# A planned attention, gated MLP and SoLU chain: slot 0 gated in one, one pair's exponentials set by set, ten weight blocks' low bits on ScalarE

## The chip, the cores and the metric

One NeuronCore of a Trainium2 chip runs the whole kernel. The metric is the device time of one execution in microseconds (us). Engines are TensorE (PE, with its weight loads as PEld), VectorE (DVE), ScalarE (ACT), GpSimd (POOL) and SyncE (SP), whose queue issues nearly all DMAs.

## The reference, cut to what matters

Three stages follow one another, for 2304 tokens of 512 features:

```python
attn = softmax(where(mask, q @ k.T / 8, -1e9)) @ v        # 4 x 8 heads, 576 positions, head size 64
x = attn as (2304, 512)                                   # plain heads: a window of 32; the others: every 4th of 128
xn = x / sqrt(mean(x * x) + 1e-6) * rms_g
g, val = xn @ w_gate, xn @ w_val                          # 512 x 1536 each
y = (silu(g) * val) @ w_out                               # 1536 x 512
h = y @ w_in                                              # 512 x 1024
solu = h * softmax(h); ln = layernorm(solu) * g_ln        # over 1024
out = ln @ w_out2                                         # 1024 x 512
```

The weights come as float64 and are turned into float32 on the chip.

## The kernel before, in words

**Tiling.** The tokens are cut into nine *pieces* of 256 (`PIECES`, L29). Pieces 0 and 1 are part 0 (512 tokens), piece 2 is part 1, and parts 2, 3 and 4 have two pieces each (`PARTS`, L34). The MLP has twelve *slots* of 128 hidden features (`f`, of `NF1`); a slot has three weight blocks of 128 x 512: gate (0), value (1), output (2). Every product is made of three float32r matmuls, high x high, high x low, low x high (`mm3`, L951), so each operand is split into a high part (a cast) and a low part (the difference).

**Who sets the order.** Nothing is ordered by hand, but for the last stages. Every step is entered with `plan.add(name, {engine: cost}, emit, needs, takes, uses, due)` (L201): engines that may run it with an estimated cost, the steps it needs, the buffers it takes, a due time. `Plan.order` (L210) plays this forward and picks, on the engine that is free first, the step with the smallest due time among those that can start within `SLACK` of the earliest. `NUDGE` (L110) shifts due times by name, `ENGINE` (L147) fixes an engine where several may serve. The instructions are then issued in that order (L1876), and on the chip each engine runs its own in order. Where the plan has TensorE idle before `FILL` = 75 us (L878), `fill` (L347) puts in matmuls on a constant tile that keep it busy and compute nothing.

**Weights.** `prepare` (L358) makes the steps of a slot: `fetch` (DMA of 512 KB per block), `shifted` (ScalarE, on the float64's high word, L386), `parts` (VectorE, the top three bits of the low word, L391), `joined` (VectorE, L395: both into one float32), `halves` (ScalarE, the cast), `lows` (VectorE or GpSimd, the difference). Slots below `SINGLE` = 7 do this block by block, the others all three blocks in one operation.

**Attention of the first two pieces.** `pair(t, m)` (L463), for t and m of 0 and 1, makes: `load_qk`, `load_v`, `scores` (32 matmuls and one that adds the mask, L493), `maximum`, `centred` (subtracts the maximum, on TensorE through an identity, L522, or on VectorE, L519), `exps` (one exponential over 128 x 512, L526), `sums` (L529), `norm`, `weights`, `transposes`, `turned0` and `turned1` (two copies out of PSUM, by `put`, L333 or L339), `values`. Then `rms(t)` (L767): `square`, `total` (matmuls with ones, L820), `eps`, `root` (GpSimd), `diag` (two operations, L858), `spread` (a matmul, L863), `keep` (piece 0), `scale`, `high` (L333 or L337) and `low` (L342). The other seven pieces go through `attention` (L599), later and beside the MLP; their `exps` is one exponential with an accumulated sum for each set of 64 keys (L660). Their `rms` adds the squares on GpSimd and then multiplies the sum by a matrix of ones (`mean`, L827, one float32 matmul of 256 columns in the code).

**The MLP.** `VIRTUAL` (L169) lists what `mlp` (L956) is called for: with `HALVES` = 1, slot 0 is done for piece 0 alone (v = 0), then for piece 1 alone (v = 1), each with gate and value products (`into`, L970), `tanh`, `silu`, `prod`, `uhigh`, `ulow` and output product (`outs`, L1012) over 256 tokens; slots 1 to 11 of part 0 are done over 512 tokens (v = 2); v = 3 and 4 are parts 1 and 2. The last two parts go together through Strassen-like products (`joint`, L1090), and the last stage works on pairs of 128-token rows (`second_stage`, L1708). `PACE` (L153) says after which gate product each later attention unit may start.

## Time and profile before

| | |
|---|---|
| runs of the kernel before | 711.76 us, median of 3 (711.76 to 712.01) |
| the profiled execution's own time | 712.27 us |
| its span in the trace | 710.2 us |
| TensorE, VectorE, ScalarE, GpSimd busy | 702.3, 509.4, 358.9, 135.5 us |

The span runs from the first to the last recorded instruction; the execution's own time has some 2 us more around it. A busy TensorE says that matmuls were under way, also those of `fill`. In the trace a matmul's record is longer than the distance to the next one's start, since matmuls overlap; that distance is what one costs in a dense run. Helpers issue instructions for many steps: L333, L337 and L339 are `put` (on ScalarE and VectorE), L342 is `less`.

### The profile page before, as it was taken

The numbers are of one execution on the slowest core, as the hardware profiler recorded it, in microseconds if no ns is written. First come the engines' busy times: TensorE is split into PE (matmuls) and PEld (weight loads), VectorE is DVE, ScalarE is ACT, GpSimd is POOL, SyncE is SP. The second block draws the span as 40 slices with busy tenths as digits, with TensorE's granted clock in tenths as the row PEclk, the third lists the DMA queues.
The fourth block names the chain that finished last, engine by engine and source line by source line (L and its number), as shares of the span: only waits on it lengthen the run. The fifth ranks groups of instructions, "written<-read, shape, count | busy, mean of one in ns | idle before, by whom it ended". The sixth has DMA issues, their size and how long they took to land.

```text
span 710.2 us, 11738 instructions
## 1 busy us (share of the span) xinstructions
PE 702.3 (99%) x4533; PEld 593.3 (84%) x4533; DVE 509.4 (72%) x932; ACT 358.9 (51%) x769; POOL 135.5 (19%) x166
## 2 busy tenths in 40 slices
PE   8999999999999999999999999999999999999998
PEld 6788888899998888888888888888888888888887
DVE  5899899679585986668966766689677677665552
ACT  2976854344535554516655554355375555543440
POOL 0322432250506121110000000014044311010110
PEclk9999999999999999999999999999999999999999
DMA  9999433154368764403321112947032111000001
GB/s 336 401 407 354 133 101 118 64 185 141 134 225 293 276 206 141 141 7 125 123 72 37 52 60 97 344 139 220 1 119 75 60 60 45 30 16 30 30 30 45
DMA packets 42424, 97.21 MB, mean 137 GB/s; under 512 B 3841, under 2 KB 14081, under 8 KB 42369
## 3 DMA queue, kind: packets, MB, share of 16 engines
q1 hardware_dynamic: 40640, 93.33, 37.9%
q10 hardware_dynamic: 1728, 3.15, 1.2%
q8 instruction: 35, 0.57, 0.3%
q14 instruction: 21, 0.16, 0.1%
HBM read 72.87 MB, written 23.59 MB: 136 GB/s over the span
## 4 chain that ended last, share of the span: by engine, by line
PE 93%; DMA 5%; ACT 1%; DVE 1%; SPq 0%; issue 0%; ACTq 0%
PE y L952 7%; PE ca L1292 7%; PE y L954 7%; PE y L953 7%; PE o L1689 5%; PE o L1688 5%; PE o L1687 5%; PE g L952 4%; PE vp L952 4%; PE g L953 4%; PE g L954 4%; PE vp L954 4%; PE vp L953 4%; DMA raw<-w 3%; PE cd L1292 2%; PE cb L1292 2%
## 5 line engine op out<-in xcount | busy, mean ns | idle before, releaser
L342 POOL TENSOR_TENSOR w<-wf,w 128x512 fp32r<-128x512 f32 (+1 forms) x15 | 25.1, 1673 | 203.9 <-ACT w L333 203.9
L1687 PE MATMUL o<-w,lt 128*128 128x512 f32 (+1 forms) x152 | 58.9, 388 | 0.0
L1689 PE MATMUL o<-w,lt 128*128 128x512 f32 (+1 forms) x152 | 57.6, 379 | 0.0
L1688 PE MATMUL o<-w,lt 128*128 128x512 f32 (+1 forms) x152 | 57.5, 379 | 0.0
L952 PE MATMUL y<-uh,w 128*128 128x512 f32 (+1 forms) x148 | 53.2, 359 | 0.0
L954 PE MATMUL y<-uh,w 128*128 128x512 f32 (+1 forms) x148 | 51.7, 349 | 0.0
L953 PE MATMUL y<-uh,w 128*128 128x512 f32 (+1 forms) x148 | 51.7, 349 | 0.0
L660 ACT ACTIVATE s<-s,nm 128x64 f32<-128x64 f32 x120 | 40.1, 337 | 18.6 <-DVE nm L655 18.6
L333 ACT CAST w<-wf 128x512 fp32r<-128x512 f32 (+1 forms) x40 | 28.3, 728 | 25.5 <-DVE wf L395 11.5
L952 PE MATMUL g<-xh,w 128*128 128x512 f32 (+1 forms) x104 | 40.4, 389 | 0.0
L333 ACT CAST uh<-u 128x512 fp32r<-128x512 f32 (+1 forms) x37 | 19.9, 537 | 38.3 <-DVE u L996 37.7
L953 PE MATMUL g<-xl,w 128*128 128x512 f32 (+1 forms) x104 | 39.0, 375 | 0.2 <-DVE xl L342 0.2
L952 PE MATMUL vp<-xh,w 128*128 128x512 f32 (+1 forms) x100 | 39.0, 390 | 0.0
L954 PE MATMUL g<-xh,w 128*128 128x512 f32 (+1 forms) x104 | 38.9, 374 | 0.0
L954 PE MATMUL vp<-xh,w 128*128 128x512 f32 (+1 forms) x100 | 38.2, 382 | 0.0
L953 PE MATMUL vp<-xl,w 128*128 128x512 f32 (+1 forms) x100 | 38.1, 381 | 0.0
L805 POOL TENSOR_TENSOR sq<-x 128x256 f32<-128x256 f32 x28 | 17.8, 647 | 105.7 <-DVE x L337 61.6
L1655 POOL TENSOR_SCALAR st<-st 128x1 f32<-128x1 f32 x18 | 8.7, 484 | 140.5 <-ACT sq L1646 140.3
L992 DVE SCALAR_TENSOR_TENSOR u<-u,g 128x512 f32<-128x512 f32 (+1 forms) x37 | 21.5, 582 | 18.3 <-ACT u L986 18.3
L986 ACT ACTIVATE u<-g 128x512 f32<-128x512 f32 (+1 forms) x37 | 19.0, 514 | 27.9 <-PE g L954 27.2
L1689 PEld LDWEIGHTS o<-w,lt 128*128 128x128 f32 x152 | 28.6, 188 | 5.3
L342 DVE TENSOR_TENSOR lt<-tp,lt 128x512 fp32r<-128x512 f32 x36 | 23.2, 684 | 13.6 <-ACT lt L333 13.6
(290 smaller groups left out, 2056.5 us busy)
## 6 DMA issues: line engine op xcount, KB each, us to landing
raw<-w SPq DMA_DIRECT2D x36, 512.0 KB, 9.1
es<-ec SPq DMA_DIRECT2D x12, 512.0 KB, 3.1
sc<-es SPq DMA_DIRECT2D x12, 512.0 KB, 3.4
qk<-qk SPq DMA_DIRECT2D x7, 800.0 KB, 5.5
vt<-v SPq DMA_DIRECT2D x10, 512.0 KB, 5.6
wo<-w SPq DMA_DIRECT2D x9, 512.0 KB, 7.6
wst<-wo SPq DMA_DIRECT2D x9, 512.0 KB, 3.7
yT<-yo SPq DMA_DIRECT2D x16, 256.0 KB, 3.1
```

The costliest lines, as they stand in the source:

```text
L333: nc.scalar.copy(dst, src) if scale is None else nc.scalar.mul(dst, src, scale)
L342: ENG[e].tensor_tensor(dst, a, b, ALU.subtract)
L660: nc.scalar.activation(T[s_][:, i], T[s_][:, i], AF.Exp, bias=st["nm"][:, i:i + 1], accum_out=sm[:, i:i + 1])
L952: nc.tensor.matmul(acc, wh, xh, start=first, stop=False)
L953: nc.tensor.matmul(acc, wh, xl, start=False, stop=False)
L954: nc.tensor.matmul(acc, wl, xh, start=False, stop=last)
L986: return lambda e: nc.scalar.activation(new(up, ("u", v, f), [P, 512])[:, 0:n], T["g", v, f], AF.Tanh, scale=0.5)
L992: return lambda e: nc.vector.scalar_tensor_tensor(out=u_of(f), in0=u_of(f), scalar=1.0, in1=T["g", v, f], op0=ALU.add, op1=ALU.mult)
L1292: nc.tensor.matmul(acc(x), w, y, start=not more and j == 0 and n == 0, stop=j == 1 and n == 2, skip_group_check=True)
L1687: nc.tensor.matmul(o, lt[:, 0, k], w[:, 0], start=(k == 0), stop=False)
L1688: nc.tensor.matmul(o, lt[:, 0, k], w[:, 1], start=False, stop=False)
L1689: nc.tensor.matmul(o, lt[:, 1, k], w[:, 0], start=False, stop=(k == NF2 - 1))
```

## The change

`HALVES` and the virtual tiles 0 and 1 are gone: slot 0 of part 0 belongs to v = 2. Its gate and value products run piece by piece (`by_piece`), the rest of the slot over 512 tokens. Pair (0, 0) scales its negated maximum by 1/8 on ScalarE and takes eight exponentials with accumulated sums; it has no `centred` and no `sums`. The mask's matmul is a step of its own (`masked`). `parts` may run on ScalarE, as one multiplication with a bias that rounds to the same three bits. Weights go block by block for slots 0 and 1, blocks 0 and 1 together for slots 2 to 6, all three from slot 7 on. `mean` of pieces 2 to 8 splits the sum of squares into high and low and uses two float32r matmuls. Estimated costs are changed in many places, the due times of a great many steps too (`NUDGE` grows from some 130 entries to some 270), `PACE` lets several attention units start earlier, and a few buffers of the last stages move (`units`, `H_AT`). Of `NUDGE` only the entries that the text speaks of stand here.

```diff
-HALVES = 1
+BY_SET = ((0, 0),)
...
-SINGLE = 7
+APART, WIDE = 2, 7
+
+
+def cuts(f):
+    return [(0,), (1,), (2,)] if f < APART else [(0, 1), (2,)] if f < WIDE else [(0, 1, 2)]
...
-         ('landed', 6): -22, ('load_qk', (1, 1)): -1.6, ('load_v', (0, 0)): 3.07, ('low', 0, 1): -43.6,
+         ('keep', 0): -197, ('landed', 6): -22, ('load_qk', (1, 1)): -1.6, ('load_v', (0, 0)): 1.8,
+         ('load_v', (0, 1)): 0.3, ('low', 0, 1): -43.6, ('low', 1, 0): -8, ('low', 1, 1): -32.8,
...
 ENGINE = {('copy', (3, 0)): 'd', ('copy', (5, 0)): 'd', ('copy', (7, 0)): 'd', ('copy', (7, 1)): 'd',
-          ('copy', (8, 1)): 'a', ('ecomb', 0): 'p', ('ecomb', 1): 'p', ('ecomb', 11): 'd', ('ecomb', 8): 'p',
-          ((1, 4), 'lows', 0): 'p', ((1, 6), 'lows', 1): 'p'}
+          ('copy', (8, 0)): 'a', ('copy', (8, 1)): 'a', ('diag', 0): 'a', ('ecomb', 0): 'p', ('ecomb', 1): 'p',
+          ('ecomb', 11): 'd', ('ecomb', 2): 'p', ('ecomb', 4): 'p', ('ecomb', 7): 'p', ('ecomb', 8): 'p',
+          ('high', 0, 0): 'a', ('high', 0, 1): 'a', ('keep', 0): 'a', ('low', 0, 0): 'p', ('low', 1, 0): 'd',
+          ('reload', 4): 'a', ('s5', 2): 'a', ('sumlow', 4): 'p', ('sums', 3): 'd', ('turned0', (1, 0)): 'a',
+          ('turned1', (1, 1)): 'a', ('u2', 2): 'a', (('in', 0), 't1'): 'p', (('in', 0), 't2'): 'd',
+          (('in', 0), 't4'): 'd', (('in', 1), 'lows', 't1'): 'p', (('in', 1), 'lows', 't3'): 'p',
+          (('in', 1), 't1'): 'd', (('in', 1), 't3'): 'p', ((1, 0), 'lows', 2): 'p', ((1, 0), 'parts', 0): 'a',
+          ((1, 0), 'parts', 1): 'a', ((1, 1), 'parts', 2): 'a', ((1, 2), 'parts', 0): 'd', ((1, 4), 'lows', 0): 'p',
+          ((1, 4), 'parts', 0): 'd', ((1, 7), 'lows', 0): 'p', ((1, 7), 'parts', 0): 'a', ((1, 8), 'parts', 0): 'a',
+          ((1, 9), 'lows', 0): 'p'}
...
-VIRTUAL = [(0, 0, 256, range(HALVES)), (0, 256, 256, range(HALVES)), (0, 0, 512, range(HALVES, NF1)),
-           (1, 0, 256, range(NF1)), (2, 0, 512, range(NF1))]
+VIRTUAL = {2: (0, 0, 512, range(NF1)), 3: (1, 0, 256, range(NF1)), 4: (2, 0, 512, range(NF1))}
...
         def parts(c):
-            return lambda e: nc.vector.tensor_scalar(word(c, 0).bitcast(U32), word(c, 0).bitcast(U32), 29, None,
-                                                     ALU.logical_shift_right)
+            def emit(e):
+                x = word(c, 0).bitcast(U32)
+                if e == "a":
+                    nc.scalar.activation(x, x, AF.Identity, scale=2.0 ** -29 * (1 - 2.0 ** -16), bias=down)
+                else:
+                    nc.vector.tensor_scalar(x, x, 29, None, ALU.logical_shift_right)
+            return emit
...
-            plan.add((key, "parts", n), {"d": one}, parts(c), [(key, "fetch", i) for i in c], due=due)
+            plan.add((key, "parts", n), {"d": one, "a": act}, parts(c), [(key, "fetch", i) for i in c], due=due)
...
         def exps(e):
-            nc.scalar.activation(T[s_], T[sp], AF.Exp, scale=0.125)
+            if K not in BY_SET:
+                nc.scalar.activation(T[s_], T[sp], AF.Exp, scale=0.125)
+                return
+            new(stg, s_, [P, 8, 64], name="s")
+            nc.scalar.mul(st["nm"], st["nm"], 0.125)
+            sm = small("sm")
+            for i in range(8):
+                nc.scalar.activation(T[s_][:, i], T[sp][:, i], AF.Exp, scale=0.125, bias=st["nm"][:, i:i + 1], accum_out=sm[:, i:i + 1])
...
         def mean(e):
             x = bank(a_mean, [P, TP], "ms")
-            nc.tensor.matmul(x, ones, T["sq", t, ks[0]], start=True, stop=True)
+            for h in range(2):
+                nc.tensor.matmul(x, ones_r, T["sqh" if h == 0 else "sql", t], start=h == 0, stop=h == 1)
+
+        def sum_high(e):
+            put(e, new(at, ("sqh", t), [P, TP], F32R, name="sqh"), T["sq", t, ks[0]])
+
+        def sum_low(e):
+            less(e, new(at, ("sql", t), [P, TP], F32R, name="sql"), T["sq", t, ks[0]], T["sqh", t])
...
-            plan.add(step("mean"), {"t": 0.45}, mean, [step("add", ks[-1]), ("ones",)], takes=[("a", a_mean)],
+            plan.add(step("sumhigh"), {"a": 0.42}, sum_high, [step("add", ks[-1])], takes=[("sq", ("sqh", t))],
                      uses=[("sq", t, ks[0])], due=due)
+            plan.add(step("sumlow"), {"p": 0.8, "d": 0.4}, sum_low, [step("sumhigh")], takes=[("rs", ("sql", t))],
+                     uses=[("sq", t, ks[0]), ("sqh", t)], due=due)
+            plan.add(step("mean"), {"t": 0.25}, mean, [step("sumlow"), ("onesr",)], takes=[("a", a_mean)],
+                     uses=[("sqh", t), ("sql", t)], due=due)
...
-                    alone = v == 4 and f == 0 and part == 0
-                    plan.add(name, {"t": cost}, by_piece(part, f, (key, v, f), i) if alone else into(part, f, (key, v, f), ks),
...
+                    alone = f == 0 and (v == 2 or v == 4 and part == 0)
+                    if alone and part == 1:
+                        before = [("g", v, f, i)] + ([(key, v, f, 0)] if i else [])
+                    plan.add(name, {"t": 1.44 if alone else cost}, by_piece(part, f, (key, v, f), i) if alone else into(part, f, (key, v, f), ks),
...
```

## Rows read from the trace of the kernel before

**Rows 1.** The page: busy time by engine; TensorE's granted clock in forty slices.

```profile
PE 702.3 (99%) x4533; PEld 593.3 (84%) x4533; DVE 509.4 (72%) x932; ACT 358.9 (51%) x769; POOL 135.5 (19%) x166
...
PEclk9999999999999999999999999999999999999999
```

**Rows 2.** Stretches: length, busy us (count) of PE, PEld, DVE, ACT, POOL; clock, DMA.

```profile
10.00:20.00 10.00, 8.59 (x144) 5.86 (x144) 8.91 (x19) 4.64 (x9) 0.00 (x0) 1.00 1.04 392
20.00:30.00 10.00, 9.22 (x127) 8.11 (x122) 8.31 (x21) 9.72 (x20) 2.31 (x2) 1.00 1.03 405
30.00:37.00 7.00, 6.35 (x50) 5.45 (x50) 5.85 (x12) 6.33 (x13) 3.33 (x3) 1.00 1.03 397
37.00:50.00 13.00, 13.00 (x81) 11.67 (x80) 12.60 (x21) 8.81 (x16) 3.98 (x3) 1.00 1.03 407
50.00:80.00 30.00, 30.00 (x216) 24.71 (x215) 28.34 (x44) 21.85 (x44) 8.35 (x6) 1.00 0.75 283
```

**Rows 3.** Groups by shape, TensorE to 75 us: the fills.

```profile
L351 PE MATMUL warm<-seed 128*128 128x256 bf16 x50 | 8.3, 323 | 0.9 <-POOL half L1870 0.9
...
L351 PE MATMUL rs<-seed 128*128 128x256 bf16 x19 | 2.5, 275 | 0.0
```

**Rows 4.** TensorE's waits from 36 us on: sum, times, longest.

```profile
PE tp L675 <- DVE s L668: 0.5, 1, 0.5
PE g L953 <- DVE xl L342: 0.2, 1, 0.2
```

**Rows 5.** Timeline of TensorE at piece 2's mean: start, length, what.

```profile
107.42 0.39 PE L954 MATMUL y<-uh,w 128*128 128x512 f32 x1
107.65 0.59 PE L827 MATMUL ms<-sq,ones 128*128 128x256 f32 x2
107.89 0.58 PE L952 MATMUL g<-xh,w 128*128 128x512 f32 x1
108.31 0.39 PE L953 MATMUL g<-xl,w 128*128 128x512 f32 x1
```

**Rows 6.** Timeline of TensorE in slot 0's first output product.

```profile
39.52 0.28 PE L952 MATMUL y<-uh,w 128*128 128x256 f32 x1
39.64 0.28 PE L953 MATMUL y<-uh,w 128*128 128x256 f32 x1
```

**Rows 7.** Timelines of the four engines in the ramp, by time.

```profile
10.27 0.67 DVE L529 TENSOR_REDUCE sm<-s 128x8 f32<-128x512 f32 x1
...
16.67 1.15 PE L566 MATMUL pv<-xp,qkv 128*64 128x64 f32 x32 [1.25 <-DMA qkv<-v]
...
17.85 0.69 ACT L386 ACTIVATE raw<-raw 128x512 f32<-128x512 f32 x1 [1.88 <-DMA raw<-w]
...
18.41 0.68 ACT L333 ACTIVATE xp<-tp,half 128x512 f32<-128x512 f32 x1
...
24.81 0.48 DVE L858 TENSOR_SCALAR rd<-ident,r 128x128 f32<-128x128 f32 x2 [0.60 <-POOL r L853]
...
30.85 1.57 DVE L858 TENSOR_SCALAR rd<-ident,r 128x128 f32<-128x128 f32 x2 [0.25 <-POOL r L853]
...
30.87 1.28 POOL L342 TENSOR_TENSOR xl<-xp,xh 128x512 fp32r<-128x512 f32 x1
...
34.69 0.68 ACT L386 ACTIVATE raw<-raw 128x512 f32<-128x512 f32 x1 [0.38 <-DMA raw<-w]
...
35.92 1.29 DVE L342 TENSOR_TENSOR xl<-x,xh 128x512 fp32r<-128x512 f32 x2 [0.71 <-ACT xh L333]
```

**Rows 8.** Groups by shape, 10 to 100 us: count, busy us, mean ns of one.

```profile
L386 ACT ACTIVATE raw<-raw 128x512 f32<-128x512 f32 x21 | 13.6, 677 | 4.3 <-DMA raw<-w 4.1
...
L391 DVE TENSOR_SCALAR raw<-raw 128x512 uint32<-128x512 uint32 x21 | 8.4, 423 | 0.4 <-DMA raw<-w 0.3
L386 ACT ACTIVATE raw<-raw 128x1536 f32<-128x1536 f32 x5 | 7.9, 1637 | 0.0
...
L660 ACT ACTIVATE s<-s,nm 128x64 f32<-128x64 f32 x16 | 5.4, 346 | 2.1 <-DVE nm L655 2.1
```

More of the change, by code (lines that the diff above doesn't have):

```diff
@@ L257, in order @@
             if e == "p" and free["d"] > start:
-                free["d"] += 0.45 * cost
+                free["d"] += (0.45 if any(str(x).endswith(("low", "lows")) for x in name) else 0.12) * cost
             done[name] = (e, start + cost)
@@ L495, in scores, with masked @@
             fill(x.rearrange("p s k -> p (s k)"))
+            for y in range(2):
+                for i in range(4):
+                    for c in range(2):
+                        b = 4 * (i // 2) + 2 * c + i % 2
+                        k0 = 512 + g["offs"][b]
+                        nc.tensor.matmul(x[64 * c:64 * c + 64, 4 * y + i, :], qk()[:, y, 64 * b:64 * b + 64],
+                                         qk()[:, y, k0:k0 + 64], start=y == 0 and i == 0, stop=False)
+        def masked(e):
+            x = T[sp]
             n = g["mask"]
@@ L503, in scores @@
                 mask_ = masks_t[:, None, P + 64 * n:P + 64 * n + 128].to_broadcast([P, 4, 128])
-            for y in range(2):
-                for i in range(4):
-                    for c in range(2):
-                        b = 4 * (i // 2) + 2 * c + i % 2
-                        k0 = 512 + g["offs"][b]
-                        nc.tensor.matmul(x[64 * c:64 * c + 64, 4 * y + i, :], qk()[:, y, 64 * b:64 * b + 64],
-                                         qk()[:, y, k0:k0 + 64], start=y == 0 and i == 0, stop=False)
             nc.tensor.matmul(into, identb, mask_, start=False, stop=True)
@@ L758, in attention @@
             needs_, takes_, uses_ = for_values(K)
-            plan.add(step("values"), {"t": 0.27 + 0.465 * N}, values, needs_, takes=takes_, uses=uses_, due=due)
-        cost = 0.7 if N == 2 and g["kind"] != "tail" else 0.5 * N
-        plan.add(step("copy"), {"d": cost, "a": cost}, copy,
+            plan.add(step("values"), {"t": 0.2 + 0.485 * N}, values, needs_, takes=takes_, uses=uses_, due=due)
+        a, d = (0.62, 0.7) if g["kind"] == "plain" else (0.85, 1.05) if N == 2 else (0.65, 0.6)
+        plan.add(step("copy"), {"d": d, "a": a}, copy,
                  [step("values") if K not in LEADS else ("scores", LEADS[K])] + ([("copy", (t, 0))] if m else []) +
@@ L1041, in mlp @@
                         before = [("g", v, f, 1)]
-                    if part == 0 and i == 0 and (f > fs[0] or v in (1, 2)):
-                        before = [("vp", v, f - 1, 1) if f > fs[0] else ("vp", v - 1, HALVES - 1, 1)]
-                    alone = v == 4 and f == 0 and part == 0
-                    plan.add(name, {"t": cost}, by_piece(part, f, (key, v, f), i) if alone else into(part, f, (key, v, f), ks),
-                             before + [made[1, f, part]] + ([(x, k, pieces[i]) for x in ("high", "low") for k in range(2)] if alone else
+                    if part == 0 and i == 0 and f > fs[0]:
+                        before = [("vp", v, f - 1, 1)]
+                    alone = f == 0 and (v == 2 or v == 4 and part == 0)
+                    if alone and part == 1:
+                        before = [("g", v, f, i)] + ([(key, v, f, 0)] if i else [])
+                    plan.add(name, {"t": 1.44 if alone else cost}, by_piece(part, f, (key, v, f), i) if alone else into(part, f, (key, v, f), ks),
+                             before + [made[1, f, part]] + ([(x, k, pieces[i]) for x in ("high", "low") for k in range(2)] if alone and part == 0 else [] if alone else
                                                             ready[i] if f == fs[0] and part == 0 else []),
@@ L1709, in second_stage @@
         add = plan.add
-        mm, base = 0.2265, 6000
+        mm, base = 0.2271, 6000
         def switch(e):
@@ L1841, in tile_attention_glu_solu @@
     plan.add(("ones",), {"d": 0.2}, lambda e: nc.vector.memset(ones, 1.0), due=-9)
+    plan.add(("onesr",), {"d": 0.2}, lambda e: nc.vector.tensor_copy(ones_r, ones), [("ones",)], due=-8)
     for t in range(len(PIECES)):
@@ L1855, in tile_attention_glu_solu @@
                 ([("low", k, 0) for k in range(2)] + [("values", K) for K in EARLY] if f == X_AT else []))
-    for v in range(len(VIRTUAL)):
+    for v in VIRTUAL:
         mlp(v, 1000 * (v + 1))
```

188 lines of the change are left out of this document (107 added, 81 removed), and 4 rows, old and new, of the table NUDGE.

## The prediction

> **What bounds the kernel now.** I read the page's busy shares first: TensorE is busy for 702.3 of 710.2 us and its clock is granted in full in all forty slices [rows 1]. That says where the bound is, not whether the work in it is useful. The view by stretches splits it: up to 37 us TensorE stands still now and then, and from 37 to 80 us it is busy for every microsecond, with VectorE beside it at 12.60 of 13 and 28.34 of 30 us and ScalarE at only 8.81 and 21.85 [rows 2]. The view by shape shows what the early "busy" is worth: 69 matmuls on a constant tile, which compute nothing, took 8.3 and 2.5 us [rows 3]. The list of TensorE's waits after 36 us has only two: 0.5 us once in 675 us, and 0.2 us at the very end of the ramp [rows 4]. So there are two kinds of time to win: matmul time after 37 us, where every 0.1 us removed is 0.1 us off the end, and the start of the dense part, which stands at 36.66 us, when VectorE delivers the low half of the second piece.
>
> **The change, part by part.**
>
> *The means of seven pieces.* `mean` of pieces 2 to 8 multiplies float32 squares by ones. The row at 107.65 us holds its two passes; from there to the start of the second matmul behind them is 108.31 - 107.65 = 0.66 us, in which one ordinary 512-column matmul (107.42 to 107.65: 0.227 before rounding) is also issued, so the mean costs 0.43 us [rows 5]. After the change it is two float32r matmuls of 256 columns. Such a step takes 0.12 us (39.52 to 39.64) [rows 6], so 0.24 us. Saved: 7 x 0.19 = 1.33 us, all in the dense part. The new `sumhigh` (ScalarE) and `sumlow` (GpSimd or VectorE) are 256 columns each, some 0.4 us, and hang between the additions and the mean; I cost them at nothing, because after 80 us VectorE and ScalarE have room and the mean is needed long before its piece is. If that cover fails, a mean stands first in TensorE's order and the matmuls behind it wait for up to the two steps, about 1 us a piece.
>
> *Slot 0 in one.* The first slot was computed as two virtual tiles of 256 tokens; now gate and value products still run by piece (24 + 24 matmuls of 256 columns, as before), but the gating and the output product run over 512. The output goes from 24 x 0.120 = 2.88 us [rows 6] to 12 x 0.227 = 2.72 us [rows 5]: 0.15 us saved. The first output product also comes later, so the gate product of slot 1 is the next thing TensorE wants after slot 0's value products. Its weights then have to be split earlier, while those of the output block can wait: an exchange of two blocks, costed at nothing. Cover gone, that is one `lows`, 0.7 us.
>
> *First pair's exponentials set by set.* VectorE loses the subtraction and the sum of pair (0,0), the latter 0.67 us at 10.27, in the middle of an unbroken run [rows 7]. ScalarE gets eight exponentials of 0.346 us [rows 8] instead of one, so the pair's weights come no earlier; ScalarE was idle in most of that time (4.64 of 10 us busy from 10 to 20) [rows 2]. Only a gain where VectorE is next late; I count it below.
>
> *Low bits on ScalarE.* The table of fixed engines names nine of the ten blocks: three single (blocks 0 and 1 of slot 0, block 2 of slot 1) and two whole slots (7 and 8). On VectorE a block takes 0.423 us, on ScalarE, by the same shape of `shifted`, 0.677, and a whole slot 1.64 [rows 8]. So ScalarE gets 3 x 0.68 + 2 x 1.64 = 5.3 us and VectorE is rid of about 9 x 0.42 = 3.8 at most (a whole slot in one is somewhat cheaper). ScalarE does an operation that reads, scales and writes the same bytes as `shifted`, so I take its duration, with 0.42 (VectorE's price) and 0.69 (the block at 17.85) [rows 7] as bounds; the turn at 18.41, which like the new operation takes a per-partition operand, has 0.68. The two whole slots fall after 60 us, where ScalarE is idle for a quarter of the time. What hides the three early blocks is room made by putting off `shifted` for later slots, which nothing needs until their slot's turn; cover gone, they cost 2.0 us on the chain (rival 3).
> By the row, moving an operation to the slower engine costs 0.25 us more per block and nothing at the end, as long as ScalarE has room. The Trainium skill, page "ScalarE: Activation LUTs", section "Rules for kernel authors", would keep plain arithmetic on VectorE; by that rule alone the ten blocks are a loss of 10 x 0.25 = 2.5 us and the sum would be 1.5 us, which is also rival 1's price; the rows agree with it on the price of one operation, and leave open whether it is on the path.
>
> *The order in the ramp.* The loads of V for pairs (0,0) and (0,1) change places (due -2.9 and -4.3 before, -4.2 and -4.0 after), and splitting, diagonal and copies are given to fixed engines. Read against the timeline [rows 7]: TensorE stood 1.25 us ahead of `values` of pair (0,0) for V, and the centring of pair (1,1), the chain that ends the ramp, was queued behind it. ScalarE stood 1.88 us for a weight block at 17.85 with a turn of weights queued behind. At 30.85 VectorE's two diagonals took 1.57 us while GpSimd ran the low half beside them; the new table gives that low half to VectorE. At 34.69 ScalarE waited for a weight block and shifted it before the high half of piece 1, 0.38 + 0.68 us in which the high half was queued, and VectorE then stood 0.71 us for it; I count 0.9, between the two. I take 1.25 + 0.4 (1.57 less the 0.48 of the two at 24.81, less 0.65 for the low half on VectorE, half of the two at 35.92) + 0.9 = 2.5 us. Bounds: nothing, or even a loss, if ScalarE's added 2 us land on that chain; at most the 10.8 us of fills [rows 3], many of which run before the first load has landed. 2.5 is nearer the low end because VectorE and ScalarE are busy 23.1 and 20.7 of the 27 us from 10 to 37 [rows 2].
> A ramp that ends 2.5 us sooner must be fed: VectorE has 2.1 us spare from 37 to 80, and the parts that leave it give more than it lacks.
>
> **The sum.** 1.33 + 0.15 + 2.5 = 4.0 us off the profiled execution's 712.27, so 708.3. The median of the runs shown, 711.76, lies 0.5 us below that execution, so 707.8 us for a median. Waits in the dense part: 0.7 us before, taken as unchanged, with -0.5 and +2 as bounds, since nearly every due time is new.
>
> **Rivals.**
> 1. *Only the matmul time arrives.* The ramp is rearranged but ends where it did, because ScalarE takes over as its bound. For: from 20 to 30 us it is busy 9.72 of 10 [rows 2]. Against: much of that is shifting blocks nobody needs yet. Price: 1.5 us, 710.3.
> 2. *The ramp shrinks much more,* by 6 us, since three lags, TensorE's, VectorE's and ScalarE's, go together: 704.3. For: 10.8 us of fills [rows 3]. Against: the load of V and the busy shares above.
> 3. *ScalarE's queue holds up the attention: slower.* The queue is in order, and a block now has two operations on it that wait for the same transfer. If the three early blocks stand as the one at 17.85 did (1.88 us) and bring 2.0 us of work, the chain of piece 1 ends 3.9 us later, and with 1.5 saved later on the kernel is 2.4 us slower: 714.2. It decides from the point where those blocks are ahead of a turn or a high half before they have landed. Against: an operation that follows `shifted` waits no second time.
> 4. *The change does not do what it says:* the new due times give other orders after 80 us, with waits of up to 0.5 us like the one found [rows 4], several of them; the gain then shrinks to about 1 us, 710.8.
>
> **How the numbers follow.** Forecast 0.55; rival 1 0.17; rival 2 0.12; rival 3 0.09; rival 4 0.07. A measurement of this kernel tells 0.2 per cent, 1.4 us, from no change, so faster means below 710.3. The forecast and rival 2 are faster but for a small part (0.64), rival 1 sits on the border and gives half (0.09), rival 4 little (0.02): 0.75. Same is the rest of 1 and 4 and a little of 3, 0.16; slower 0.09. The range leaves out the far half of rival 2 and rival 3: from 704.6 to 711.2.
>
> **What would show it.** Right: the mean as two float32r matmuls with the next but one about 0.47 us after its start; the first 512-column gate product at about 37 us instead of 39.52 + 12 x 0.12 = 40.96; no 1.25 us ahead of the first `values`; three `sums` of the first two pieces in place of four. Wrong: a ramp that ends at 36 us or later (rivals 1 and 3, the second with ScalarE waits for weight blocks), or waits of TensorE on ScalarE or VectorE between 37 and 310 us above 1 us in all (rival 4).

## The result and the profile after

The changed kernel takes 719.59 us (median of 4 runs, 718.55 to 720.20) beside 711.88 us for the kernel before on the same chip (711.76 to 712.84): a ratio of 1.0104, 95% interval 1.0086 to 1.0121. It is 7.7 us slower; the prediction was 707.8 us, and its range ended at 711.2. The profiled execution took 720.1 us with a span of 718.3 us, 8.1 us more than the span of before. Medians here and below leave out three executions that lie far above the others of their kernel (one of before at 874.91 us, one of b_pad128 at 1710.08, one of a_act at 1175.24), and since the latter two are the profiled ones, no row of b_pad128 or a_act is shown.

The page's busy times, and the same stretches as [rows 2]:

```profile
PE 709.0 (99%) x4546; PEld 594.3 (83%) x4546; DVE 506.5 (71%) x924; ACT 376.2 (52%) x800; POOL 118.0 (16%) x145
```

```profile
10.00:20.00 10.00, 9.75 (x169) 7.88 (x167) 9.09 (x20) 7.66 (x23) 0.00 (x0) 1.00 1.04 412
20.00:30.00 10.00, 9.09 (x107) 7.64 (x108) 7.75 (x16) 7.62 (x15) 2.18 (x3) 0.83 0.83 311
30.00:37.00 7.00, 6.57 (x54) 5.48 (x51) 5.00 (x12) 5.62 (x11) 2.39 (x2) 1.00 1.02 410
37.00:50.00 13.00, 12.66 (x72) 11.23 (x73) 10.89 (x17) 10.29 (x17) 1.35 (x1) 1.00 1.03 414
50.00:80.00 30.00, 29.93 (x160) 24.33 (x160) 29.04 (x36) 25.70 (x44) 5.05 (x2) 1.00 0.78 302
```

The work moved as it was told to: ScalarE has 17.3 us more than before and VectorE 2.9 less, GpSimd 17.5 less. But TensorE has 6.7 us *more*, with nearly the same products (and 98 fills in place of 69), and from 20 to 30 us the mean granted clock is 0.83 and the DMA engines are busy for 0.83 of the time (1.00 and 1.03 before, [rows 2]). Set against the trace of before, the difference lies in four places.

**The means and the first exponentials did what was forecast.** Timeline of TensorE at the first mean, and at `values` of pair (0, 0):

```profile
15.47 0.74 PE L619 MATMUL pv<-xp,qkv 128*64 128x64 f32 x18
...
116.81 0.28 PE L884 MATMUL ms<-sqh,ones_r 128*128 128x256 f32 x1
116.92 0.28 PE L884 MATMUL ms<-sql,ones_r 128*128 128x256 f32 x1
```

The two steps of the mean start 0.11 us apart and take 0.25 us together on the average of the seven, where [rows 5] had 0.43. `values` no longer waits for V and starts at 15.47 in place of 16.67 [rows 7]. VectorE runs three `sums` in the first two pieces instead of four.

**The ramp ends later.** Timelines of TensorE, ScalarE and VectorE around the second piece, then a line of TensorE and one of VectorE in the kernel before, and the longest wait of SyncE's queue from 8 to 42 us (sum, times, longest):

```profile
29.33 2.18 PE L389 MATMUL rs<-seed 128*128 128x256 bf16 x18
...
31.78 2.63 PE L389 MATMUL g<-seed 128*128 128x256 bf16 x22
...
36.62 0.38 PE L1019 MATMUL g<-xh,w 128*128 128x256 f32 x1 [0.42 <-ACT xh L371]
37.34 0.38 PE L1020 MATMUL g<-xl,w 128*128 128x256 f32 x1 [0.34 <-DVE xl L380]
...
38.75 0.28 PE L1019 MATMUL vp<-xh,w 128*128 128x256 f32 x1
...
41.63 0.40 PE L1019 MATMUL g<-xh,w 128*128 128x512 f32 x1
```

```profile
33.52 0.75 ACT L432 ACTIVATE raw<-raw,down 128x512 uint32<-128x512 uint32 x1
35.39 0.68 ACT L424 ACTIVATE raw<-raw 128x512 f32<-128x512 f32 x1 [1.12 <-DMA raw<-w]
35.97 1.12 ACT L371 CAST xh<-x 128x512 fp32r<-128x512 f32 x2
```

```profile
30.61 0.51 DVE L377 TENSOR_SCALAR rd<-ident,r 128x128 f32<-128x128 f32 x2
...
31.98 1.65 DVE L942 SCALAR_TENSOR_TENSOR x<-x,rmsg,rs 128x256 f32<-128x256 f32 x4 [0.25 <-PE rs L926]
...
36.60 1.29 DVE L380 TENSOR_TENSOR xl<-x,xh 128x512 fp32r<-128x512 f32 x2 [1.76 <-ACT xh L371]
```

```profile
33.73 0.28 PE L952 MATMUL vp<-xh,w 128*128 128x256 f32 x1
```

```profile
33.22 1.66 DVE L879 SCALAR_TENSOR_TENSOR x<-x,rmsg,rs 128x256 f32<-128x256 f32 x4 [0.19 <-PE rs L863]
```

```profile
SPq L409 <- PE pv L619: 5.5, 1, 5.5
```

Read them from the end: TensorE waits for the low half, VectorE stands 1.76 us for the high half (0.71 before, [rows 7]), and ScalarE had run a low-bit step of slot 3 (0.75 us) and stood 1.12 us for a weight block of slot 1, both queued ahead of that high half. The two diagonals take 0.51 us, as forecast, instead of 1.57, and the scaled piece 1 is ready at 33.63 us (31.98 + 1.65), 1.25 us sooner than before (33.22 + 1.66); but ScalarE takes up its high half only at 35.97, so what had been gained up to there was lost in ScalarE's queue. SyncE stood 5.5 us for `values`: the first of three early fetches of slots 9 and 10 goes into a tile that the attention still holds, and everything queued behind it had to wait. And the order on TensorE is new: the twelve value products of piece 0, which before began at 33.73, ahead of piece 1, begin at 38.75, behind the gate products of piece 1, since the value block of slot 0 is now the last of its three. In all, gate and value products of slot 0 are done at 41.63, where before the same work was done at 39.52 (the first output product of [rows 6]): 2.1 us later, where 2.5 us earlier had been predicted. Of these, 0.7 are the low half (TensorE's second product on piece 1 starts at 37.34 instead of 36.66 us), and 1.4 are the twelve value products behind it (12 x 0.12).

**The dense part waits more.** TensorE's waits from 36 us on:

```profile
PE tp L731 <- DVE s L724: 1.2, 3, 0.8
PE g L1019 <- ACT xh L371: 0.4, 1, 0.4
PE cd L1362 <- ACT cd L1369: 0.4, 1, 0.4
PE g L1020 <- DVE xl L380: 0.3, 1, 0.3
PE g L1019 <- DVE u L1056: 0.3, 1, 0.3
```

2.6 us in place of 0.7 [rows 4]; the two on `xh` and `xl` are the end of the ramp.

**The same matmuls take longer.** This is the largest part, and the list of waits does not show it. Groups by shape, mean duration in ns as the last figure before the idle time, of a product of the second stage and one of the third; first before, then after:

```profile
L1292 PE MATMUL ca<-xt,shl 128*128 128x512 f32 x108 | 28.4, 389 | 0.0
...
L1614 PE MATMUL ha<-w,yh 128*128 128x512 f32 x30 | 11.7, 389 | 0.0
```

```profile
L1362 PE MATMUL ca<-xt,shl 128*128 128x512 f32 x108 | 29.1, 395 | 0.0
...
L1684 PE MATMUL ha<-w,yh 128*128 128x512 f32 x30 | 11.8, 395 | 0.0
```

Neither line was touched by the change, and the clock is granted in full there. Measured from start to start, the 512-column steps of `ca<-xt,shl` and `ha<-w,yh` went from 226.7 to about 233 ns. What all float32r steps of 256 and 512 columns take above 119.8 and 226.7 ns, counted where it is at most 20 ns, adds up to 1.0 us before and 5.4 us after; of these, 0.3 and 4.6 us lie behind 325 us, where the change touches almost nothing. What did change there is where the tiles lie: the new constant `down` has 4 bytes a partition and takes 32, so that every later tile on the left side moved by 32 bytes, while the right-hand tiles, which are laid out from the other end, stayed.

The parts: placement +4.4, ramp +2.1, waits behind the ramp +1.4 (1.9 in place of 0.5), means -1.3, merged output -0.15: 6.45 us of the 8.1. For the other 1.6 us no single place was found; some 1.0 of them lie ahead of the second stage, whose first product starts at 327.29 us instead of 324.55.

### The profile page after: what moved, and what is told of

Read it like the earlier page. It is cut to its first block, busy times and chain, and to the rows that moved or that the text cites. A ratio compares the mean times of both kernels' runs of the same rounds, so it can differ in the third digit from the quotient of the medians.

```text
span 718.3 us, 11753 instructions
## 1 busy us (share of the span) xinstructions
PE 709.0 (99%) x4546; PEld 594.3 (83%) x4546; DVE 506.5 (71%) x924; ACT 376.2 (52%) x800; POOL 118.0 (16%) x145
## 4 chain that ended last, share of the span: by engine, by line
PE 84%; DVE 8%; ACT 3%; DMA 3%; issue 1%; SPq 0%; DVEq 0%; ACTq 0%
PE ca L1362 6%; PE y L1019 6%; PE y L1021 6%; PE y L1020 6%; PE o L1759 5%; PE o L1757 5%; PE o L1758 5%; PE vp L1019 3%; PE g L1019 3%; PE vp L1021 3%; PE vp L1020 3%; PE g L1020 3%; PE g L1021 3%; PE tp L1738 2%; PE cd L1362 2%; PE cc L1362 2%
## 5 line engine op out<-in xcount | busy, mean ns | idle before, releaser
L1019 PE MATMUL y<-uh,w 128*128 128x512 f32 (+1 forms) x144 | 52.1, 362 | 0.0
L1021 PE MATMUL y<-uh,w 128*128 128x512 f32 (+1 forms) x144 | 51.1, 355 | 0.0
L1020 PE MATMUL y<-uh,w 128*128 128x512 f32 (+1 forms) x144 | 51.0, 354 | 0.0
L861 POOL TENSOR_TENSOR sq<-x 128x256 f32<-128x256 f32 x28 | 17.5, 635 | 104.4 <-DVE x L375 54.3
L371 ACT CAST w<-wf 128x512 fp32r<-128x512 f32 (+2 forms) x35 | 27.6, 803 | 11.8 <-PE y L1021 5.3
L380 POOL TENSOR_TENSOR w<-wf,w 128x512 fp32r<-128x512 f32 (+2 forms) x10 | 23.7, 2378 | 58.3 <-ACT w L371 58.3
L1759 PEld LDWEIGHTS o<-w,lt 128*128 128x128 f32 x152 | 28.6, 188 | 5.6
L380 DVE TENSOR_TENSOR uh<-u,uh 128x512 fp32r<-128x512 f32 (+1 forms) x36 | 29.5, 823 | 5.1 <-ACT uh L371 5.0
L1758 PEld LDWEIGHTS o<-w,lt 128*128 128x128 f32 x152 | 28.7, 189 | 5.0
```

What stands on the lines that cost most here:

```text
L371: nc.scalar.copy(dst, src) if scale is None else nc.scalar.mul(dst, src, scale)
L380: ENG[e].tensor_tensor(dst, a, b, ALU.subtract)
L861: ENG[e].tensor_tensor(sq, xk, xk, ALU.mult)
L1019: nc.tensor.matmul(acc, wh, xh, start=first, stop=False)
L1020: nc.tensor.matmul(acc, wh, xl, start=False, stop=False)
L1021: nc.tensor.matmul(acc, wl, xh, start=False, stop=last)
```

## The experiments

Each time stands beside runs of the kernel before on the same chip (medians 711.8 to 712.2).

**Placement, on the kernel before.** A constant that nobody reads is put in ahead of the other tiles, and nothing else: 32, 64, 128 and 256 bytes.

```diff
+    pad = const.tile([P, 8], F32, name="pad")    # 16, 32, 64 in the other three
...
+    nc.vector.memset(pad, 0.0)
```

> The kernel before with one unused constant of 32 bytes a partition (set once by VectorE, read by nobody). Every left-hand tile moves by 32 bytes, as in the changed kernel; the right-hand tiles stay; the instructions and their order are those of before. Theory of placement (TensorE steps whose operand addresses are of both kinds, 0 and 32 over a multiple of 64 bytes, take about 5 to 8 ns more, in sum some 5 us): 711.9 + 5 = 716.9 us, the 512-column steps of the product with yh at about 232 ns. Rival (only the order and the engines of the work count): 711.9, within 0.5.

> The same with an unused constant of 64 bytes: all tiles keep their remainder by 64. Theory of placement: no change, 711.9 within 0.5. Rival 1 (only order counts): 711.9 as well. Rival 2 (any shift of the addresses or any added tile costs): as the 32-byte kernel, some 717.

> The kernel before with an unused constant of 128 bytes a partition, since 64 bytes cost 2.7 us where no change was expected, so the remainder by 64 is not the whole rule. All tiles keep their remainder by 128. Theory A (what counts is that all operands share their remainder by 128): 712.1, under 50 slow steps more than before. Theory B (by 256 or more): some 714 to 716. Theory C (any shift of the left-hand tiles costs): 715.

> The same with 256 bytes. Theories A and B (remainders by 128 or 256): 712.1. Theory C (any shift): 715. If this one is slow and the 128-byte one isn't, neither holds.

Measured: 715.37 us with 32 bytes (ratio 1.0041, 1.0027 to 1.0056), 714.85 with 64 (1.0037, 1.0024 to 1.0050), 715.30 with 128 (1.0043, 1.0028 to 1.0058), 711.86 with 256 (1.0000, 0.9991 to 1.0010). The first of the two groups with 32, 64 and 256 bytes, in this order:

```profile
L1293 PE MATMUL ca<-xt,shl 128*128 128x512 f32 x108 | 29.1, 395 | 0.0
```

```profile
L1293 PE MATMUL ca<-xt,shl 128*128 128x512 f32 x108 | 28.9, 393 | 0.0
```

```profile
L1293 PE MATMUL ca<-xt,shl 128*128 128x512 f32 x108 | 28.4, 389 | 0.0
```

The first theory, the remainder by 64, was too narrow: 32 bytes cost 3.3 us, and a shift by 64 or 128 bytes costs about as much, though for 64 no cost had been expected. The 5 us of the expectation were too much; the excess of the steps, counted as above, is 4.2 us more with 32 bytes than before. Of the four shifts only 256 bytes is free. So, as far as these four show, it is the remainder by 256 that the operands have to share. The addresses of the compiled programs, set beside the start-to-start times of their 512-column float32r steps, say the same ("shared" when the moving tile, its weights and the next step's weights have one remainder by 256):

```
kernel          shared: steps, mean ns, at 230 ns or more    mixed: steps, mean ns, at 230 ns or more
before                  2306    227.1    156                     0
32 bytes                1830    227.7    319                   476    233.4    465
64 bytes                1830    227.9    342                   476    230.4    277
256 bytes               2306    227.1    156                     0
changed                 1837    227.8    347                   480    233.4    469
changed, same64         2313    227.1    168                     4
```

The mixed steps are slow nearly without exception where 0 and 224 meet (465 of 476 and 469 of 480), and in more than half of the cases where 32 and 224 meet (277 of 476). Some of the others are slow as well (156 become over 300); for those no rule was found.

**Placement, on the changed kernel (a_same64).** The bias moves into a free column of an older constant.

```diff
-    down = const.tile([P, 1], F32, name="down")
+    down = mhalf[:, 3:4]
```

> The changed kernel with its 4-byte bias kept in a free column of an older constant instead of a tile of its own, so that all tiles have the remainder by 64 of before; nothing else differs. Theory of placement: 719.6 - 5.0 = 714.6 us; what then stays over 711.9 is 2.1 of the ramp and about 1.9 of added waits, less 1.3 of the means. Rival (the order of the work is the whole loss): 719.6.

Measured: 715.47 us, ratio 1.0042 (1.0027 to 1.0057) where the changed kernel had 1.0104 (1.0086 to 1.0121). The same two groups:

```profile
L1362 PE MATMUL ca<-xt,shl 128*128 128x512 f32 x108 | 28.4, 389 | 0.0
...
L1684 PE MATMUL ha<-w,yh 128*128 128x512 f32 x30 | 11.7, 389 | 0.0
```

4.1 us of the loss are four bytes. The rest of the experiments on the changed kernel start from this one, and ask for the 3.4 us that stay.

**The ramp's causes, singly and together.** Emission order alone is edited, with one helper, `behind(name, *moved)`, which puts steps behind another one in the list that the planner gives.

```diff
# a_sp
+        behind(((1, 1), "fetch", 0), ((1, 9), "fetch", 0), ((1, 9), "fetch", 2), ((1, 3), "fetch", 2),
+               ((1, 10), "fetch", 1))
+        behind(("load_qk", (0, 1)), ("ident",))
# a_act
+        behind(("high", 1, 1), ((1, 3), "shifted", 1), ((1, 3), "parts", 1), ((1, 1), "shifted", 0))
# a_spact: both
# a_partsd
+        order = [(a, n, x, "d" if x[1:2] == ("parts",) else k) for a, n, x, k in order]
```

> The changed kernel with the addresses of before (715.5 us), and on SyncE's queue four fetches of blocks of slots 3, 9 and 10 put behind the first block of slot 1, and ident behind the second pair's load; nothing else is moved. Theory (SyncE stands about 4 us for tiles that the attention still holds, and the blocks of slots 0 and 1 land late; this holds up ScalarE and the high halves): 1 to 2 us less, 713.5 to 714.5, with a DMA share of 20 to 30 us back at about 1.0. Rival (the ramp is set by the queues of VectorE and ScalarE, whenever the blocks land): 715.5.

> The changed kernel with the addresses of before (715.5 us), and on ScalarE's queue three steps on blocks (shifted and parts of slot 3, shifted of slot 1's first block) put behind the last high half of piece 1; SyncE as in the changed kernel. Theory (the three, one of them waiting about 1.1 us for its transfer, hold up the high halves, as the prediction's rival 3 had it): VectorE's 1.6 us wait for xh goes, 0.8 to 1.5 us less, 714.0 to 714.7. Rival (the weights of slot 0 are what is late): 715.5.

> The changed kernel with the addresses of before, and both moves made before singly: the fetches on SyncE (714.5) and the three block steps on ScalarE (714.6). Theory (two causes in a row, each on the path of its own): 713.6. Rival (one chain, which either move frees, after which another step is last): 714.4 to 714.7.

> The changed kernel with the addresses of before (715.5), every low-bit step back on VectorE at the same place of the order. Theory (the engine of the low bits is not what the ramp waits for; ScalarE and VectorE exchange some 3 us of work before 42 us): 715.5 within 0.7. Rival 1 (ScalarE's added work is the ramp's loss, as the prediction's rival 3 had it): about 1.5 us less, 714.0. Rival 2 (VectorE is the bound and the move pays): 716.5 or more.

Measured: a_sp 714.52 us (1.0036, 1.0022 to 1.0049), a_act 714.59 (1.0038, 1.0024 to 1.0052), both 714.95 (1.0040, 1.0024 to 1.0056), parts on VectorE 716.10 (1.0059, 1.0044 to 1.0074). The single moves gave some 0.9 us, about the least that had been expected, and their intervals overlap with that of a_same64; together they gave no more, which is what the rival of a_spact said (714.4 to 714.7; measured 0.25 us above that). The engine of the low bits hardly matters, and undoing that part of the change gains nothing: the Trainium skill, page "ScalarE: Activation LUTs", section "Rules for kernel authors", would keep such plain arithmetic on VectorE, and by the prediction's reckoning of it up to 2.5 us should have come back here; the run, 0.6 us slower with overlapping intervals, does not show that.

**Slot 0's value block (a_swap, a_swap2, a_swap2_sp, a_swap2_d).** The steps of value and output block change names, and the value products of piece 0 go ahead of the gate products of piece 1.

```diff
+        def swapped(n):
+            return n[:2] + (3 - n[2],) if n[0] == (1, 0) and n[2] in (1, 2) else n
+        order = [(a, i, swapped(x), k) for a, i, x, k in order]
+        behind(("g", 2, 0, 0), ("vp", 2, 0, 0))
# a_swap2 and the two behind it: planned times of the moved products, from which the fills are counted
+        ends = {("vp", 2, 0, 0): 37.0, ("g", 2, 0, 1): 38.45}
+        order = [(ends.get(x, a), i, x, k) for a, i, x, k in order]
```

> The changed kernel with the addresses of before (715.5), with the value and output blocks of slot 0 exchanged in every step that prepares them, and the value products of piece 0 ahead of the gate products of piece 1 in TensorE's order. Theory (in the changed order the value block is the last of slot 0, so that 24 products of 0.12 us that could run while piece 1 is turned come after it): 1.5 to 2.5 us less, 713.0 to 714.0, the first 512-column gate product at about 39 us in place of 41.18. Rival (piece 1 itself is late): within 0.5 of 715.5.

> The same exchange with the four fetches and ident put back on SyncE's queue as in the run that did this alone (714.5). Theory (the late value block and the late fetches are two causes): 712 to 713. Rival (they are one): as the better of the two, 713.5 to 714.5.

> As the exchange of slot 0's value and output blocks, but without the 21 extra matmuls on the constant tile that the loop had put ahead of the moved products (16 of them stood 1.7 us before the value products at 36.4, and 8 more 0.8 us later). Theory (piece 1 comes at the same time in both kernels, and the ramp's loss is the 12 value products of piece 0, 1.44 us, that ran before it in the kernel before and behind it in the changed one): the first 512-column gate product at 39.2 to 39.8 in place of 41.18, the time 713.5 to 714.1. Rival (piece 1 or the blocks are late whatever the order): 715.5 within 0.5.

> The same with the four fetches and ident put back on SyncE's queue. Theory (the fetches are a cause of their own): 712.5 to 713.2. Rival (one cause, or TensorE's clock falls in the ramp as in the earlier run of both, 0.50 from 30 to 33 us): 713.5 or more, with a granted clock under 1.00 between 20 and 37 us.

> The exchange without the extra matmuls, and the low bits of all blocks on VectorE. Theory (the engine of the low bits moves the ramp by under 0.7 us): 713 to 714.5. Rival (once the value products are back in front, VectorE, which gets some 3 us of work before 42 us, is the bound): 715 or more.

Measured: a_swap 717.39 us (1.0086, 1.0068 to 1.0103), a_swap_sp 716.55 (1.0068, 1.0051 to 1.0084), a_swap2 716.41 (1.0062, 1.0047 to 1.0077), a_swap2_sp 714.03 (1.0031, 1.0021 to 1.0040), a_swap2_d 715.63 (1.0050, 1.0033 to 1.0067). The theory missed in all five. The first two carried 21 more matmuls on the constant tile ahead of the moved products; without these a_swap2 is still no faster than a_same64, and a_swap2_d is not clear of it either. Only with the fetches put right does the exchange come out 1.4 us ahead of a_same64, with overlapping intervals, and a_sp had 714.52 without it: a gain from the exchange itself is not shown. What stands in its way can be read in the ramp of a_swap2_sp: TensorE's timeline, VectorE's longest wait, and the stretches with the granted clock (third figure from the end).

```profile
28.24 3.79 PE L389 MATMUL rs<-seed 128*128 128x256 bf16 x18
31.86 0.61 PE L926 MATMUL rs<-rd,ones 128*128 128x256 f32 x2
32.30 2.63 PE L389 MATMUL g<-seed 128*128 128x256 bf16 x22
34.68 0.36 PE L1019 MATMUL g<-xh,w 128*128 128x256 f32 x1
```

```profile
DVE x L942 <- PE rs L926: 1.9, 1, 1.9
```

```profile
27.00:30.00 3.00, 2.56 (x17) 2.02 (x18) 2.88 (x9) 3.00 (x7) 2.14 (x3) 0.74 1.02 400
30.00:33.00 3.00, 3.00 (x19) 2.29 (x18) 1.10 (x3) 2.47 (x5) 1.73 (x1) 0.69 1.02 407
```

The granted clock falls to its lower level (1.2 in place of 2.4 GHz) between 27 and 33 us, behind a stretch of few matmuls (16 from 24 to 27 us, where the kernel before runs 47); that this is why it fell is not shown, for a_fewer runs 44 there and falls too. The number of fills is fixed when the kernel is built, from planned times; at half clock the 18 ahead of the second `spread` take 3.79 us instead of 2.18, and VectorE, whose diagonals were ready at 30.0, stands 1.9 us behind them. In this trace, what lands sooner is given back there.

**Fewer fills (a_fewer).** a_swap2_sp with 4 fills for 18, and 8 for 22.

```diff
                 filling[0] = int((at_ - free) / (0.13 if free else 0.25)) if at_ < FILL else 0
+                filling[0] = min(filling[0], {("spread", 1): 4, ("g", 2, 0, 0): 8}.get(name, 99))
```

> The exchange of the blocks and the fetch order together (714.0), and of the matmuls on the constant tile 4 in place of 18 ahead of the second spread, and 8 in place of 22 ahead of slot 0's first product. Theory (these stand in TensorE's order ahead of work that is ready; at half clock the 18 took 3.8 us and VectorE stood 1.9 us behind them, so that whatever lands sooner is not used): VectorE's wait for rs under 0.5 us, the first 512-column gate product at 39 to 39.5 in place of 40.86, the time 712.0 to 712.8. Rival 1 (fewer of them let the clock fall further or for longer, and the products of slot 0 run at half speed): 714 or more with a granted clock under 1.00 from 30 to 40 us. Rival 2 (VectorE's queue is as late by itself): 714.0 within 0.4.

Measured: 713.94 us (1.0024, 1.0013 to 1.0036).

```profile
DVE x L942 <- PE rs L926: 0.7, 1, 0.7
```

```profile
30.00:37.00 7.00, 6.19 (x34) 5.20 (x34) 6.29 (x14) 6.99 (x12) 2.33 (x2) 0.65 0.95 355
```

The theory's three figures were all missed, and the time is that of rival 2. The wait behind the fills did shrink, from 1.9 to 0.7 us, and the first 512-column gate product came at 40.35 instead of 40.86; but, as rival 1 said, the clock was low for longer, the eight fills ahead of slot 0 still took 1.91 us, and the time stayed. The variants of the ramp side by side (before: slot 0's gate and value work done at 39.52, clock 1.00 throughout). The first two columns of numbers are read from one execution each, whose own time is the third; the last is the median:

```
kernel        slot 0's gate and value done   lowest clock of a 3 us stretch, 18 to 39 us   that execution   median
a_same64                41.18                       0.58                                 715.17           715.47
a_sp                    40.73                       0.60                                 713.49           714.52
a_spact                 42.08                       0.50                                 715.85           714.95
a_partsd                40.58                       1.00                                 715.44           716.10
a_swap                  41.69                       1.00                                 715.64           717.39
a_swap_sp               44.88                       0.50                                 718.73           716.55
a_swap2                 42.91                       0.50                                 717.56           716.41
a_swap2_sp              40.86                       0.69                                 713.94           714.03
a_swap2_d               41.85                       0.55                                 716.69           715.63
a_fewer                 40.35                       0.50                                 713.94           713.94
```

No variant brings the ramp back to 39.52. The traces show three things one behind the other (the order in which the blocks land, the order of slot 0's products, the fills with the clock), and undoing one shows the next; what share of the 1.7 us each has could not be told apart, and stays open.

**Two terms of the prediction, on the kernel before (b_terms).**

```diff
+        behind(("load_v", (0, 0)), ("load_v", (0, 1)))
+        behind(("high", 1, 1), ((1, 1), "shifted", 0))
```

> The kernel before with two moves that the prediction had priced in the ramp, and nothing else: V of pair (0,0) is loaded ahead of V of pair (0,1), and the shift of slot 1's first block goes behind the last high half of piece 1 on ScalarE. Theory (the prediction's prices, 1.25 and 0.9 us, both on the chain that ends the ramp): 711.9 - 2.1 = 709.8. Rival (the ramp ends with the weights, which land no sooner): 711.9 within 0.5.

Measured: 712.94 us (1.0013, 1.0003 to 1.0023). TensorE's waits from 8 to 37 us, first before, then here:

```profile
PE pv L566 <- DMA qkv<-v: 1.3, 1, 1.3
...
PE sp L509 <- DMA qkv<-qk: 0.5, 1, 0.5
...
PE pv L566 <- ACT xp L333: 0.2, 1, 0.2
```

```profile
PE sp L509 <- DMA qkv<-qk: 1.4, 2, 1.0
...
PE pv L566 <- ACT xp L333: 0.8, 1, 0.8
```

The wait for V is gone, and 0.9 us of waiting for scores and 0.6 for turned weights have come instead. The second move worked where it was made: the low half of piece 1 starts at 35.31 instead of 35.92, without the 0.71 us [rows 7]. But nine fills began at 35.30 and took 1.18 us, so TensorE used only part of it: slot 0's first output product came at 39.20 instead of 39.52, 0.3 us for a price of 2.15. In the same trace the second stage starts 1.1 us sooner than before (323.46 instead of 324.55 us), 0.5 of which is the wait for `s` of [rows 4], which is not there. The median does not show this gain, and that goes with the clock: the ten times spread from 710.89 to 713.94 us, the two lowest (0.7 us under the lowest of before) with a mean granted clock of 1.000, the six highest with 0.992 to 0.995. Where it fell in those executions no profile shows.

**The means alone (b_mean, b_mean2).** First as planned steps, then with everything else held in the order of before.

```diff
# both
-            nc.tensor.matmul(x, ones, T["sq", t, ks[0]], start=True, stop=True)
+            for h in range(2):
+                nc.tensor.matmul(x, ones_r, T["sqh" if h == 0 else "sql", t], start=h == 0, stop=h == 1)
# b_mean: sumhigh and sumlow by plan.add, as in the change
# b_mean2: put into the planned list, 0.9 and 1.5 us behind the last addition
+                order += [(x[0] + 0.9 + 0.6 * i, x[1], ("sum", i, x[2]), "ap"[i]) for i in range(2)]
```

> The kernel before with one part of the change alone: the means of pieces 2 to 8 as two float32r products (sumhigh, sumlow and a second constant of ones), all other operands at the addresses of before and the ramp's order the same. Theory (the prediction's first term: 7 x 0.19 us, the new steps hidden): 711.9 - 1.3 = 710.5. Rival 1 (the mean waits for sumhigh and sumlow): 711.9 or more, with TensorE waits on them. Rival 2 (a share of the float32 passes was hidden): 711.4.

> The kernel before with the new means alone, and this time the order of everything else written down as before: only sumhigh and sumlow are put in, 0.9 and 1.5 us behind a piece's last addition, and the mean and the steps behind it moved by at most 1.3 us. Theory (the 8 us of the run with the planned means came from the new order behind 325 us, not from the means): 711.9 - 1.3 = 710.5, the range 710.2 to 711.0. Rival (float32r means cost the stages behind them): 711.9 or more.

Measured: b_mean 720.01 us (1.0117, 1.0102 to 1.0133), b_mean2 714.07 (1.0029, 1.0019 to 1.0039). TensorE's longest wait in b_mean from 320 to 350 us, its wait for VectorE ahead of that, the stretch behind 325 us, then the largest wait of b_mean2 from 60 to 325 us:

```profile
PE ce L1304 <- issue: 4.3, 1, 4.3
```

```profile
PE g L964 <- DVE u L1004: 1.6, 2, 1.1
```

```profile
325.00:340.00 15.00, 10.16 (x35) 7.68 (x34) 14.78 (x22) 8.10 (x14) 0.00 (x0) 0.84 0.41 140
```

```profile
PE ms L830 <- POOL sql L344: 0.8, 2, 0.4
```

b_mean neither gains nor loses up to 325 us (the first `ca<-w,w` at 324.54, as before at 324.55): its means take 0.29 us each, 1.0 us less in all, and 1.6 us of waiting for `u` have come in. Then it loses 9.3 us up to the first product with `yh`: the planner, given two new steps a piece, orders the work ahead of the second stage anew. The last mean stands at 318.86 us instead of 309.11, VectorE has the steps behind it to do when the second stage begins and comes to the `shl` that TensorE wants at 334.41 instead of 325.50, TensorE stands 4.3 us, and the clock falls behind that. With the order held, b_mean2 shows what is left: the two steps of a mean take 0.54 us on the average (3.81 over 7), more than the 0.43 of before, since GpSimd's `sumlow` is late for two of them, and other waits have moved. Both expectations of a gain failed. That the median of b_mean2 is 2.0 us above before, and its profiled execution (713.02, the lowest of 8) only 0.8 above that of before, is not explained.

No version's median beat the kernel before.

## Why the prediction was wrong

**What was left out: the placement.** "The change part by part" prices every instruction, and none of its terms is a tile. The line `down = const.tile([P, 1], F32)` is in the diff, and it is 4.4 of the 8.1 us in the trace and 4.1 of the 7.7 in the runs. No rival held it either. The steps are small enough to look like nothing (3 per cent of a fifth of the 512-column steps), and the page does not show them; the view by shape, group by group, does.

**The ramp, "1.25 + 0.4 + 0.9 = 2.5 us".** The three local readings were right in two cases: `values` without the wait, the diagonals at 0.51. The third went the other way: ScalarE stood for a weight block ahead of the high half for 1.12 us where it had been 0.38. That is rival 3's mechanism, more in the wait for the block than in the one low-bit step ahead of it; it had been given a chance of 0.09. The step that failed is the addition: the sum took three waits at different places of one chain as if each ended at TensorE, and b_terms shows two of them worth 0.3 us at the end of the ramp: behind each stood another transfer, a turn, or fills. And the sentence "an exchange of two blocks, costed at nothing" has the other half: twelve products of 0.12 us lost their place ahead of piece 1.

**The means, "7 x 0.19", with "sumhigh" and "sumlow" costed at nothing.** On TensorE the term arrived, 0.25 us for a mean; that the kernel is 1.3 us shorter for it no run shows, and alone it gained nothing in b_mean and b_mean2. The bound given for a failing cover, a mean that stands first in TensorE's order, is what b_mean2 shows.

**Waits in the dense part, "taken as unchanged, with -0.5 and +2 as bounds".** They grew by 1.9 (1.4 behind the ramp), inside the bounds; rival 4 was right here, and b_mean shows what its mechanism can cost: more than the whole change.

**ScalarE for low bits.** Priced at nothing at the end, and a_partsd shows no difference that could be told. The price of one was too low: 0.75 to 0.83 us in the ramp, where 0.68 was taken.

The signs that the text named were the right ones to look at: the first 512-column gate product at 41.63, the ramp's end behind 36 us, ScalarE's wait for a block. They account for 2 us of 8. Without the placement the kernel is still 3.4 us slower (a_same64), where 4.0 us faster had been forecast; of this the trace places 1.7 us in the ramp, and how they divide among its causes stays open.

## What to carry to other kernels

When a change adds a tile, look at the addresses before the times: an unread constant of 32 bytes cost 3.3 us here, and one of 256 nothing, so keep the operands of float32r matmuls like these at one remainder by 256, and try a change with its new tiles padded or placed in old ones. In a ramp with fills whose number is fixed in advance, a wait that is removed is only worth what the next wait in the chain leaves; move one step on the old kernel and see the end of the chain move before adding up waits. With an order that a planner gives, a new step is not local: hold the order fixed when a part is to be priced.

## What the runs showed of the hardware that was not expected

*Operand addresses and TensorE's speed.* 512-column float32r steps took 227.1 ns where all operands had the remainder 224 by 256, and 233.4 ns where tiles at 0 met tiles at 224; shifts of 32, 64 and 128 bytes cost 2.7 to 3.5 us over the kernel, 256 bytes 0.0. The Trainium skill, page "SBUF — State Buffer", section "Operand start alignment", asks only that an operand starts at a multiple of its element size, and says that its runs are about legality and timed nothing; the rows here add the time.

*The clock in the ramp.* The kernel before holds 1.00 through the whole ramp in its trace. In 45 of the 81 executions of it that stand beside the experiments the mean granted clock is 0.997 or 0.998, and their median is 0.5 us above that of the other 36 (712.15 and 711.69 us); so a fall is not peculiar to the changed kernel, whose execution with 1.000 took 719.08 us. The changed kernel fell to the lower level between 20 and 26 us, and of the variants in the table above all but a_partsd and a_swap did so somewhere between 20 and 36 us. Stretches of the changed kernel:

```profile
18.00:20.00 2.00, 1.79 (x17) 1.61 (x17) 1.86 (x6) 1.76 (x6) 0.00 (x0) 1.00 1.07 428
20.00:22.00 2.00, 1.76 (x12) 1.53 (x12) 0.93 (x3) 1.82 (x3) 0.71 (x1) 0.71 1.00 398
22.00:24.00 2.00, 2.00 (x34) 1.77 (x32) 1.35 (x2) 1.01 (x2) 0.00 (x0) 0.50 0.75 298
```

In the stretch before the fall and the one in which it comes TensorE ran 17 and 12 matmuls, many of them on one column, where the kernel before ran 31 and 28; the record still calls 3.55 of these 4 us busy. But the kernel before also ran only 17 from 24 to 26 us, busy for 1.37 of 2 us, and kept 1.00, so no rule follows from these counts.
